# Taking the attention chunks two at a time beside the logits, with four chunk places on two load queues and a shorter float64 conversion

## Chip, cores and metric

One core of one Trainium2 chip runs the whole program. The metric is device microseconds (us) of one execution; lower is better. The quoted time is the median of three timed executions; the trace comes from one further execution, which the hardware profiler recorded.

## What is computed

Three stages, each fed by the one before it. In the first, 8 batches x 8 heads of 576 positions x 64 go through linear attention with decay. In the second, the 4608 tokens of width 512 go through a gated layer with 2048 hidden units. In the third, the tokens are spread over 32 slots (softmax down the tokens), the slots go through 8 small two-layer networks, and a softmax over the slots gathers the results.

```python
scores = scale * np.matmul(q, k.transpose(0, 1, 3, 2))
ret = scores * Dmat            # gamma**(i-j) for i >= j, else 0
x = np.matmul(ret, v)          # -> [4608, 512]
h = x @ w_in;  g = h * (1.0 / (1.0 + np.exp(-1.702 * h)));  y = g @ w_out
logits = y @ phi
d = softmax(logits, over tokens);  slot_input = d.T @ y
slot_out[e] = np.maximum(slot_input[e] @ w1[e], 0.0) @ w2[e]
out = softmax(logits, over slots) @ slot_out
```

`w_in` and `w_out` reach the kernel as float64, everything else as float32.

## The kernel before

**Blocks and chunks.** The tokens go in 12 blocks of 384 (NB). A block needs six attention chunks of 64 positions (C); a chunk covers all 8 heads of one batch, and there are 72. `load_chunk` brings a chunk's q, k and v in two 256 KB DMAs, both issued by SP, into one of three `pack` tiles in turn. `chunk` then works through it: `chunk_out` multiplies on TensorE (tile `Op`), scales on VectorE (`xs`) and splits the result into a rounded and a rest part of `x` (ScalarE L205, GpSimd L206); `state` carries the running k-v product (`St`, eight small matmuls, then two VectorE products into the next pack); after that the pack's place is loaded anew for the chunk three further on, and `scores` computes the masked scores of the next chunk (`Sp`, eight small matmuls, two VectorE products). Op, Sp and St matmuls have 64 output rows each, and run in pairs.

**A block.** For each of 16 slices `fc` of the hidden units, `main_fc` does 12 matmuls of 128x384 into `hp` (L328; the three of a rounded-and-rest product, four times), ScalarE applies the gate (L330), and `turn_fc` transposes on VectorE (L351). After eight slices, 16 DMAs of 96 KB on SP regroup the transposed values into `nat` (L357). `logits_group` adds four slices' logits in four matmuls of 32 output rows each (`Lg`, L364), `softmax_part` (`lt`, `dp`) and `slots_part` (`Sg`, 12 matmuls of 32 output rows, L412) finish the block before. Blocks 1 to 11 are a loop over fc; while block n's matmuls run, the chunks of block n+1 are put in at fc 0, 2, 5, 8, 10 and 12.

**The start.** Block 0's order is the string START: T loads a chunk, A works one through, I converts a slice of w_in (`load_w_in`), O converts two of w_out and folds them with phi into `Wp` (`make_wp`), M is a slice of block 0. A float64 value is turned into a float32 by bit operations on its two halves: scale the upper half on ScalarE, shift the lower by 29 (L277, L295), shift-and-or the two (L278, L296), and put the sign back (L279 for w_in; for w_out ScalarE's Sign L293 and a product L297). The raw values go through a ring of eight places, six in `early_raw` and two in `raw`.

**The order on each engine** is not the order of the code: the instructions are put in order by a scheduler with its own clock when the program is built, so the program text says only which operations exist and what they depend on. Every engine then runs its own list in order, and SP issues its DMAs in order.

**The end.** In the last blocks SP fetches w1 and w2 (33 MB) into places that become free; then come the two layers and the result.

Of the kernel before, what the change touches and what calls it, by code (L numbers as in the profile page):

```python
# [42 lines left out]
NPACK = 3  # L43
# [67 lines left out]
def tile_kernel(ctx, tc, qkv, w_in, w_out, phi, w1, w2, consts, out):  # L111
# [45 lines left out]
    for i in range(NPACK):  # L157
        t = pa.tile([128, 7, NP, C], F32, name=f"pack{i}", bufs=1)
        pool.memset(t[0:C, 0:KN], 0.0)
        pool.memset(t[C:128, KTA:7], 0.0)  # L160
        packs.append(t)
# [75 lines left out]

    def chunk_items(n):
# [3 lines left out]
        chunk_at = CHUNK_AT_LAST if n == LAST else CHUNK_AT  # L242
        return [(chunk_at[i], lambda g=g: chunk(g)) for i, g in enumerate(range(n * NB // C, (n + 1) * NB // C))]
# [10 lines left out]
    def load_raw(src, rows):  # L254
        i = count[0]
        count[0] += 1
        if i % 8 < 6:
            raw = early_raw[:, i % 8]
        else:
            raw = px.tile([128, 1024], F32, tag="raw", name="raw", bufs=2)  # L260
# [24 lines left out]
    def make_wp(i):  # L285
        r0 = 2 * (i % 2)
        for j in range(2):
# [3 lines left out]
            if wide:  # L291
                bits, sign = wo.bitcast(I32), free
# [436 lines left out]
```

## Time and profile before

| | |
|---|---|
| timed executions | 803.54, 803.67, 805.54 us: median 803.67 |
| profiled execution | 797.39 us, of which the recorded span 795.6 us |
| TensorE busy | 727.0 us, 91% of the span |
| VectorE / ScalarE / GpSimd busy | 49% / 31% / 23% |
| granted TensorE clock, mean | 0.982 |
| DMA | 142.19 MB, 179 GB/s over the span |

The profiled execution took 6.3 us less than the median of the timed ones. Busy shares are means over stages with different limits: the start up to the first `hp` matmul at 55.2 us, block 0 up to 127.9 us, the steady blocks 1 to 10 up to 662.5 us, block 11, and the tail from 713 us.

### The profile page before, as it was taken

How to read it: one execution, taken by the hardware profiler on the slowest of the kernel's cores; microseconds unless marked ns; L12 is line 12 of the kernel's file. 1: busy time of each engine (PE TensorE's matmuls, PEld its weight loads, DVE VectorE, ACT ScalarE, POOL GpSimd, SP SyncE). 2: the span in 40 equal slices, each digit the busy share in tenths (PEclk: the TensorE clock that was granted, in tenths of full speed). 3: DMA queues.
4: the chain of work that ended last, by engine and by line, in shares of the span. 5: the costliest groups of instructions: out<-in, count | busy, mean ns of one | idle time of the engine just before them, and what ended most of it. 6: DMA issues, size and time to landing. Idle time of an engine off the chain costs nothing.

```text
span 795.6 us, 18020 instructions
## 1 busy us (share of the span) xinstructions
PE 727.0 (91%) x7288; PEld 589.8 (74%) x7288; DVE 391.0 (49%) x1152; ACT 245.4 (31%) x479; POOL 186.2 (23%) x255
## 2 busy tenths in 40 slices
PE   3359999999999999999999999998998999997994
PEld 3247788788788878887888788878877798772453
DVE  3999964545445535454454454543543542222223
ACT  2446552323123223231132232411311323431323
POOL 5664661121221121212221212121122110001000
PEclk9999899999999999999999999999999999998997
DMA  9998867575355644744555447435544559898978
GB/s 230 283 297 247 266 168 187 128 157 130 80 122 122 135 106 106 159 114 96 119 125 132 111 105 160 116 85 119 134 97 99 124 126 324 278 379 341 408 307 325
DMA packets 78003, 142.19 MB, mean 179 GB/s; under 512 B 10720, under 2 KB 52960, under 8 KB 77920
## 3 DMA queue, kind: packets, MB, share of 16 engines
q1 hardware_dynamic: 75616, 136.85, 62.8%
q10 hardware_dynamic: 2304, 4.20, 1.5%
q8 instruction: 57, 0.93, 0.5%
q14 instruction: 26, 0.21, 0.1%
HBM read 92.77 MB, written 13.63 MB: 134 GB/s over the span
## 4 chain that ended last, share of the span: by engine, by line
PE 63%; SPq 15%; DMA 9%; DVE 9%; issue 3%; ACT 1%; POOL 0%; DVEq 0%; POOLq 0%; ACTq 0%
PE hp L328 38%; SPq L357 13%; DMA pack<-in_qkv_dram 8%; PE Sg L412 4%; PE Lg L364 4%; PE Op L197 2%; PE Sp L184 2%; PE h_ps L589 2%; PE so_ps L653 2%; PE St L223 1%; DMA early_raw<-in_moe_w_in_dram 1%; PE op L671 1%; DVE early_raw L278 1%; SPq L171 1%; PE St L224 1%
## 5 line engine op out<-in xcount | busy, mean ns | idle before, releaser
L328 PE MATMUL hp<-x,w 128*128 128x384 f32 x2304 | 445.3, 346 | 2.2 <-ACT x L205 2.2
L328 PEld LDWEIGHTS hp<-x,w 128*128 128x128 f32 x2304 | 399.8, 191 | 32.8 <-issue 10.6
L330 ACT ACTIVATE gT<-hp 128x384 f32<-128x384 f32 x192 | 93.9, 490 | 299.0 <-PE hp L328 297.9
L187 POOL TENSOR_TENSOR kt<-pack,cs 64x256 f32<-64x256 f32 x128 | 83.1, 649 | 215.2 <-DMA pack<-in_qkv_dram 138.8
L351 DVE STREAM_TRANSPOSE ring<-gT 128x128 f32<-128x128 f32 x240 | 55.9, 284 | 127.1 <-ACT gT L330 127.1
L351 DVE STREAM_TRANSPOSE pre<-gT 128x128 f32<-128x128 f32 x288 | 65.4, 281 | 81.3 <-ACT gT L330 77.9
L206 POOL TENSOR_TENSOR x<-xs,x 128x256 fp32r<-128x256 f32 x72 | 56.4, 783 | 195.9 <-ACT x L205 195.1
L197 PEld LDWEIGHTS Op<-pack 128*64 128x64 f32 x576 | 42.2, 144 | 37.4 <-issue 23.8
L205 ACT CAST x<-xs 128x256 fp32r<-128x256 f32 x72 | 29.1, 405 | 126.3 <-DVE xs L204 126.1
L183 PE MATMUL Sp<-pack 128*64 128x64 f32 x576 | 51.9, 233 | 16.9 <-DMA pack<-in_qkv_dram 11.4
L197 PE MATMUL Op<-pack 128*64 128x64 f32 x576 | 53.3, 236 | 12.0 <-DVE pack L189 12.0
L183 PEld LDWEIGHTS Sp<-pack 128*64 128x64 f32 x576 | 43.2, 146 | 18.9 <-issue 11.5
L223 PE MATMUL St<-pack,kt 128*64 128x64 f32 x512 | 47.2, 234 | 9.4 <-DVE pack L227 7.8
L184 PE MATMUL Sp<-pack 128*64 128x64 f32 x576 | 50.3, 233 | 5.6 <-DMA pack<-in_qkv_dram 5.6
L198 PE MATMUL Op<-pack 128*64 128x64 f32 x576 | 51.4, 236 | 0.0
L223 PEld LDWEIGHTS St<-pack,kt 128*64 128x64 f32 x512 | 38.7, 146 | 14.5 <-POOL kt L187 8.9
L364 PE MATMUL Lg<-gT,Wp 128*32 128x384 f32 x384 | 46.5, 502 | 2.5 <-DVE Wp L312 2.5
L184 PEld LDWEIGHTS Sp<-pack 128*64 128x64 f32 x576 | 42.3, 146 | 8.0 <-DMA pack<-in_qkv_dram 7.7
L224 PE MATMUL St<-pack,kt 128*64 128x64 f32 x512 | 44.8, 234 | 0.0
L198 PEld LDWEIGHTS Op<-pack 128*64 128x64 f32 x576 | 41.6, 145 | 0.7 <-DVE pack L190 0.5
L189 DVE TENSOR_TENSOR pack<-Sp,cs 64x256 f32<-64x256 f32 x72 | 30.6, 424 | 19.7 <-PE Sp L184 13.9
L224 PEld LDWEIGHTS St<-pack,kt 128*64 128x64 f32 x512 | 37.6, 147 | 2.6 <-issue 2.6
(125 smaller groups left out, 644.4 us busy)
## 6 DMA issues: line engine op xcount, KB each, us to landing
pack<-in_qkv_dram SPq DMA_DIRECT2D x144, 256.0 KB, 4.7
wx<-in_moe_w_dram SPq DMA_DIRECT2D x56, 512.0 KB, 8.6
nat<-pre SPq DMA_DIRECT2D x192, 96.0 KB, 2.2
nat<-ring SPq DMA_DIRECT2D x160, 96.0 KB, 2.2
out_dram<-ob SPq DMA_DIRECT2D x18, 512.0 KB, 3.4
early_raw<-in_moe_w_in_dram SPq DMA_DIRECT2D x13, 512.0 KB, 9.9
early_raw<-in_moe_w_out_dram SPq DMA_DIRECT2D x11, 512.0 KB, 7.4
wo_dram<-ring ACTq DMA_DIRECT2D x16, 256.0 KB, 6.2
```

The costliest lines, as they stand in the source:

```text
L183: pe.matmul(Sp[C:128, p, :], t[:, KTA, p], t[:, Q0, p], start=True, stop=True)
L184: pe.matmul(Sp[0:C, p, :], t[:, KTB, p], t[:, Q1, p], start=True, stop=True)
L187: pool.tensor_tensor(kts[g % 2][r0:r0 + C, h], t[r0:r0 + C, KN], ksc[r0:r0 + C, cb, :].unsqueeze(2).to_broadcast([C, NP, D]), op=ALU.mult)
L197: pe.matmul(Op[0:C, p, :], t[:, V0, p], t[:, Q0, p], start=True, stop=True)
L198: pe.matmul(Op[C:128, p, :], t[:, V1, p], t[:, Q1, p], start=True, stop=True)
L223: pe.matmul(s_[0:C, p, :], kk[:, 0, p], t[:, V0, p], start=first, stop=True, skip_group_check=True)
L224: pe.matmul(s_[C:128, p, :], kk[:, 1, p], t[:, V1, p], start=first, stop=True, skip_group_check=True)
L328: pe.matmul(hp, wt[fc][:, a, dc, :], b[n][:, dc, :], start=(i == 0), stop=(i == 3 * NDC - 1))
L330: act.activation(gT[n, g][:, fl, :], hp, AF.Gelu_apprx_sigmoid)
L351: dve.transpose(dst[:, c], src[:, c])
L357: sp.dma_start(nat[n][32 * b:32 * b + 32, :, a, hf * HF:(hf + 1) * HF, :], pre[n, hf][32 * a:32 * a + 32, b])
L364: pe.matmul(Lg[n][32 * fl:32 * fl + 32, :], Wp[:, g * GF + fl, :], gT[n, g][:, fl, :], start=(g == 0), stop=(g == NFC // GF - 1))
```

## The change

1. From the third block on, chunks go in pairs: `two_chunks` at fc 4, 8 and 12 replaces the single chunks at six places, and the logits groups move from fc 6, 10, 14 to fc 4, 8, 12, where the pairs stand (LOGITS_AT 2 to 0). A pair's VectorE, ScalarE and GpSimd operations work on both chunks at once (128x512 where there were two of 128x256), the matmuls stay the same in number and size. The order within an item is St of the pair's second chunk, Op of the pair, Sp of the next pair, St.
2. Four places for packs, in two tiles of two; the loads' lower rows go by SP, the upper rows by ScalarE's queue. A pair's two places are loaded anew, four DMAs, once its Op matmuls are done. The zeroing of the first two places moves from GpSimd to VectorE.
3. The sign of a float64 is made by Prelu: with a slope of 2^32 for negative values the scaled upper half gets the exponent bit that the shift turns into the sign. L279 goes for all 16 slices of w_in; Sign and the product L297 go for all 16 of w_out.
4. The ring of raw values has seven places (`raw` one). The last prefetch has nine places in `pw2` and one in `raw`, where it had eight and two.

```diff
-NPACK = 3
+NPACK = 4
-CHUNK_AT = (0, 2, 5, 8, 10, 12)
-CHUNK_AT_LAST = (0, 3, 6, 9, 10, 13)
-LOGITS_AT, SOFTMAX_AT, SLOTS_AT = 2, 1, 4
+CHUNKS_AT = (4, 8, 12)
+LOGITS_AT, SOFTMAX_AT, SLOTS_AT = 0, 1, 4
...
         sp.dma_start(t[0:C, KN * PC:7 * PC], qkv[g, 0:C])
-        sp.dma_start(t[C:128, 0:KTA * PC], qkv[g, C:128])
+        act.dma_start(t[C:128, 0:KTA * PC], qkv[g, C:128])
...
+    def two_chunks(k):
+
+        g = 2 * k + 1
+        last = g + 1 == NT // C
+        if not last:
+            scaled_keys(g + 1)
+            state(g)
+        out_of_two(k)
+        if not last:
+            scores_of_two(k + 1)
+            state(g + 1)
+            scaled_keys(g + 2)
+        for ahead in (g + 3, g + 4):
+            if ahead < NT // C:
+                load_chunk(ahead)
...
-            act.activation(w, w, AF.Copy, scale=2.0 ** -112)
+            act.activation(w, w, AF.Prelu, scale=2.0 ** -112, alpha=2.0 ** 32)
             dve.tensor_scalar(lower, lower, 29, None, op0=ALU.logical_shift_right)
-            dve.scalar_tensor_tensor(lower, upper, 3, lower, op0=ALU.logical_shift_left, op1=ALU.bitwise_or)
-            dve.scalar_tensor_tensor(upper, upper, -2147483648, lower, op0=ALU.bitwise_and, op1=ALU.bitwise_or)
+            dve.scalar_tensor_tensor(upper, upper, 3, lower, op0=ALU.logical_shift_left, op1=ALU.bitwise_or)
...
-                act.activation(sign, upper.bitcast(F32), AF.Sign)
-                act.activation(wo, upper.bitcast(F32), AF.Copy, scale=2.0 ** -112)
+                act.activation(upper.bitcast(F32), upper.bitcast(F32), AF.Prelu, scale=2.0 ** -112, alpha=2.0 ** 32)
...
-                (pool if how["mul"][i] else dve).tensor_tensor(wo, wo, sign, op=ALU.mult)
```

**On TensorE, in a steady block**, the row of before around a logits group of block 5. `Lg` is the logits group, `hp` a slice of the block, Sp, Op and St are chunk matmuls (Op's L197 and L198, Sp's L183 and L184).

```order
L183 MATMUL Sp<-pack_93 64x64
L184 MATMUL Sp<-pack_93 64x64
L328 MATMUL hp<-x,w 128x384 x24
L364 MATMUL Lg<-gT,Wp 32x384 x4
L328 MATMUL hp<-x,w 128x384 x24
L197 MATMUL Op<-pack_93 64x64
L198 MATMUL Op<-pack_93 64x64
```

The same engine after the change, between the pairs of fc 4 and fc 8 (L387 is `hp`, L423 the logits group, L279 and L280 are St, L201 Op).

```order
L387 MATMUL hp<-x,w 128x384 x14
L423 MATMUL Lg<-gT,Wp 32x384 x3
L279 MATMUL St<-packs_93,kt_106 64x64
L280 MATMUL St<-packs_93,kt_106 64x64
L279 MATMUL St<-packs_93,kt_106 64x64
L280 MATMUL St<-packs_93,kt_106 64x64
L279 MATMUL St<-packs_93,kt_106 64x64
L280 MATMUL St<-packs_93,kt_106 64x64
L279 MATMUL St<-packs_93,kt_106 64x64
L423 MATMUL Lg<-gT,Wp 32x384
L280 MATMUL St<-packs_93,kt_106 64x64
L201 MATMUL Op<-packs_98 64x64
```

The group of four is now cut in three and one with St matmuls between. At the pair of fc 4 another group stands within the slot matmuls `Sg` (L471):

```order
L387 MATMUL hp<-x,w 128x384 x11
L471 MATMUL Sg<-nat,dn 32x512 x6
L423 MATMUL Lg<-gT,Wp 32x384 x4
L471 MATMUL Sg<-nat,dn 32x512 x6
L201 MATMUL Op<-packs_98 64x64
```

Before, the 12 stood together, with hp ahead and Op behind.

**On SP**, the loads of one and a half steady blocks before (L171 and L172 a pack's two halves, L357 the 16 regrouping DMAs):

```order
L357 DMA nat<-pre 32x3x256 x16
L171 DMA pack_93<-in_qkv_dram 64x1024
L172 DMA pack_93<-in_qkv_dram 64x1024
L171 DMA pack_96<-in_qkv_dram 64x1024
L172 DMA pack_96<-in_qkv_dram 64x1024
L172 DMA pack_99<-in_qkv_dram 64x1024
L171 DMA pack_99<-in_qkv_dram 64x1024
L357 DMA nat<-ring 32x3x256 x16
```

and after, where SP issues a pair's two lower halves as one row x2 and L416 is the regrouping (the upper halves stand on ScalarE, ahead of the pair's L245 CAST):

```order
L172 DMA packs_98<-in_qkv_dram 64x1024 x2
L416 DMA nat<-pre 32x3x256 x16
L172 DMA packs_93<-in_qkv_dram 64x1024 x2
L172 DMA packs_98<-in_qkv_dram 64x1024 x2
L416 DMA nat<-ring 32x3x256 x16
L172 DMA packs_93<-in_qkv_dram 64x1024 x2
L416 DMA nat<-pre 32x3x256 x16
L172 DMA packs_98<-in_qkv_dram 64x1024 x2
```

One load of a block still stands behind the 16 regrouping DMAs; the other halves are no longer in this list.

**On VectorE, in the start**, before (L277, L278, L279 convert w_in, L283 is the rest part, L226, L227 and L189, L190 are the chunks' products):

```order
L204 TENSOR_TENSOR xs<-Op,cs 128x256
L277 TENSOR_SCALAR early_raw<-early_raw 128x512
L278 SCALAR_TENSOR_TENSOR early_raw<-early_raw 128x512
L279 SCALAR_TENSOR_TENSOR early_raw<-early_raw 128x512
L226 TENSOR_TENSOR pack_96<-St,cs 64x256
L227 TENSOR_TENSOR pack_96<-St,cs 64x256
L189 TENSOR_TENSOR pack_96<-Sp,cs 64x256
L190 TENSOR_TENSOR pack_96<-Sp,cs 64x256
```

and after (L339 and L340 convert, L344 is the rest part):

```order
L216 TENSOR_TENSOR xs<-Op,cs 128x256
L339 TENSOR_SCALAR early_raw<-early_raw 128x512
L282 TENSOR_TENSOR packs_93<-St,cs 64x256
L283 TENSOR_TENSOR packs_93<-St,cs 64x256
L340 SCALAR_TENSOR_TENSOR early_raw<-early_raw 128x512
L196 TENSOR_TENSOR packs_93<-Sp,cs 64x256
L197 TENSOR_TENSOR packs_93<-Sp,cs 64x256
L344 TENSOR_TENSOR w<-early_raw,w 128x512
```

Each slice has one pass fewer between the chunk's products. Up to the `xs` of chunk 5 this list held 7 L279, 8 L278, 9 L277, 6 L295 and 4 L296; after the change it holds 7 L340, 7 L339, 4 L354 and 3 L355, which are L278, L277, L295 and L296 of before.

## Rows read from the trace of the kernel before

**Rows 1.** The page's first two parts: busy time of TensorE and its granted clock in tenths, in 40 slices of the span.

```profile
PE 727.0 (91%) x7288; PEld 589.8 (74%) x7288; DVE 391.0 (49%) x1152; ACT 245.4 (31%) x479; POOL 186.2 (23%) x255
...
PE   3359999999999999999999999998998999997994
...
PEclk9999899999999999999999999999999999998997
```

**Rows 2.** Windows by stage: stretch, its length, busy us of each engine (instructions), granted clock, DMA share, GB/s.

```profile
0.00:14.00 14.00, 5.08 (x64) 4.23 (x64) 2.27 (x5) 1.61 (x2) 8.21 (x18) 1.00 0.87 188
14.00:60.00 46.00, 21.22 (x254) 18.47 (x255) 43.90 (x72) 20.81 (x37) 28.70 (x25) 1.00 1.05 294
60.00:128.00 68.00, 65.07 (x797) 54.75 (x796) 57.61 (x130) 38.51 (x72) 38.16 (x38) 0.95 0.78 233
128.00:662.50 534.50, 522.66 (x5283) 440.11 (x5282) 251.46 (x860) 141.12 (x279) 108.27 (x172) 0.99 0.53 122
662.50:713.00 50.50, 50.50 (x310) 40.52 (x309) 11.26 (x25) 19.30 (x34) 0.00 (x0) 1.00 0.91 328
713.00:795.60 82.60, 62.45 (x587) 31.68 (x585) 24.46 (x63) 24.07 (x57) 2.83 (x3) 0.91 0.87 345
```

**Rows 3.** All that TensorE waited for in the steady blocks (128 to 662.5 us): total us, times, longest.

```profile
PE Sp L183 <- DMA pack<-in_qkv_dram: 7.4, 9, 1.5
PE Sp L184 <- DMA pack<-in_qkv_dram: 4.4, 6, 0.8
```

**Rows 4.** The chain of waits at one such place, 364 to 387 us (start, us, what).

```profile
364.50 0.20 PE Op L197
365.19 0.47 SPq L171
365.71 4.09 DMA pack<-in_qkv_dram
369.81 0.47 DVE pre L351 x2
370.30 0.64 SPq L357
...
381.47 0.55 SPq L171
382.12 4.00 DMA pack<-in_qkv_dram
386.16 0.27 PE Sp L184
```

**Rows 5.** Windows of the places with the clock at half, columns as in rows 2.

```profile
80.40:87.20 6.80, 6.29 (x25) 4.50 (x25) 6.71 (x14) 4.28 (x8) 4.94 (x6) 0.50 0.99 360
548.00:551.40 3.40, 3.40 (x12) 3.40 (x12) 0.37 (x1) 0.28 (x1) 1.95 (x3) 0.50 0.41 87
602.60:606.00 3.40, 3.40 (x16) 3.28 (x13) 0.84 (x2) 0.00 (x0) 1.77 (x4) 0.50 0.92 193
```

**Rows 6.** TensorE's timeline ahead of these three: start, us, what, and in brackets the idle time before it.

```profile
80.91 1.49 PE L364 MATMUL Lg<-gT,Wp 128*32 128x384 f32 x4 [2.46 <-DVE Wp L312]
...
545.72 0.30 PE L183 MATMUL Sp<-pack 128*64 128x64 f32 x2 [1.51 <-DMA pack<-in_qkv_dram]
546.78 0.27 PE L184 MATMUL Sp<-pack 128*64 128x64 f32 x1 [0.76 <-DMA pack<-in_qkv_dram]
```

**Rows 7.** Groups of instructions of the start (0 to 140 us): total us, mean ns.

```profile
L297 POOL TENSOR_TENSOR ring<-ring 128x512 f32<-128x512 f32 x14 | 20.0, 1445 | 14.8 <-ACT ring L293 7.8 <-DVE raw L295 2.4 <-DVE Wp L312 2.3
L279 DVE SCALAR_TENSOR_TENSOR early_raw<-early_raw 128x512 int32<-128x512 int32 x13 | 10.7, 822 | 0.1
L295 DVE TENSOR_SCALAR early_raw<-early_raw 128x512 int32<-128x512 int32 x11 | 10.4, 942 | 0.1
L278 DVE SCALAR_TENSOR_TENSOR early_raw<-early_raw 128x512 int32<-128x512 int32 x13 | 9.9, 759 | 0.4 <-ACT early_raw L276 0.3
L296 DVE SCALAR_TENSOR_TENSOR ring<-ring,early_raw 128x512 int32<-128x512 int32 x11 | 8.8, 815 | 1.0 <-ACT ring L294 1.0
L277 DVE TENSOR_SCALAR early_raw<-early_raw 128x512 int32<-128x512 int32 x13 | 7.4, 570 | 2.3 <-DMA early_raw<-in_moe_w_in_dram 2.3
L276 ACT ACTIVATE early_raw<-early_raw 128x512 f32<-128x512 f32 x13 | 8.8, 674 | 16.7 <-DMA early_raw<-in_moe_w_in_dram 15.6 <-DMA pack<-in_qkv_dram 1.0
L160 POOL MEMSET pack<- 64x768 f32 x3 | 2.2, 732 | 0.1
```

**Rows 8.** Timelines of VectorE and then of TensorE around the first `hp` matmul.

```profile
54.27 0.42 DVE L204 TENSOR_TENSOR xs<-Op,cs 128x256 f32<-128x256 f32 x1
...
55.19 0.69 PE L328 MATMUL hp<-x,w 128*128 128x384 f32 x1 [2.15 <-ACT x L205]
```

**Rows 9.** TensorE's timeline at a run of 12 `hp` and a whole logits group behind it, a chunk's eight Op matmuls, a run of 24 `hp`, a single logits matmul, and the 12 of `Sg` (32-row and 64-row matmuls are recorded in two passes each: a whole group as 8, a single logits matmul as 2, `Sg` as 24).

```profile
344.33 2.36 PE L328 MATMUL hp<-x,w 128*128 128x384 f32 x12
346.62 0.85 PE L364 MATMUL Lg<-gT,Wp 128*32 128x384 f32 x8
347.40 2.35 PE L328 MATMUL hp<-x,w 128*128 128x384 f32 x12
349.69 0.27 PE L197 MATMUL Op<-pack 128*64 128x64 f32 x1
...
350.20 0.28 PE L223 MATMUL St<-pack,kt 128*64 128x64 f32 x2
...
372.57 4.44 PE L328 MATMUL hp<-x,w 128*128 128x384 f32 x24
...
376.94 0.85 PE L364 MATMUL Lg<-gT,Wp 128*32 128x384 f32 x8
...
662.79 0.83 PE L364 MATMUL Lg<-gT,Wp 128*32 128x384 f32 x2
663.56 0.62 PE L328 MATMUL hp<-x,w 128*128 128x384 f32 x2
...
361.72 2.78 PE L412 MATMUL Sg<-nat,dn 128*32 128x512 f32 x24
364.43 0.27 PE L197 MATMUL Op<-pack 128*64 128x64 f32 x1
```

**Rows 10.** The chunk loads of the page's part on DMA issues: count, KB each, median us from issue to landing.

```profile
pack<-in_qkv_dram SPq DMA_DIRECT2D x144, 256.0 KB, 4.7
```

More of the change, by code (lines that the diff above doesn't have):

```diff
@@ L156, in tile_kernel @@
     packs = []
[L157 to L161, printed above, removed]
+    for i in range(NPACK // 2):
+        two = pa.tile([128, 2, 7, NP, C], F32, name=f"packs{i}", bufs=1)
+        for j in range(2):
+            own = pool if i else dve
+            own.memset(two[0:C, j, 0:KN], 0.0)
+            own.memset(two[C:128, j, KTA:7], 0.0)
+            packs.append(two[:, j])
+        both = [*both, two] if i else [two]
     kts = []
@@ L201, in chunk_out @@
             xh[n], xl[n] = x[:, 0], x[:, 1]
-        cols_ = slice(off, off + C)
-        xs = pa.tile([128, NP, C], F32, tag="xs", name="xs")
-        dve.tensor_tensor(xs, Op, osc, op=ALU.mult)
-        act.copy(xh[n][:, :, cols_], xs)
-        pool.tensor_tensor(xl[n][:, :, cols_], xs, xh[n][:, :, cols_], op=ALU.subtract)
+        return xh[n], xl[n]
+    def chunk_out(g):
+        n, off = divmod(g * C, NB)
+        Op = ps.tile([128, NP, C], F32, tag="r", name="Op", bufs=3)
+        out_products(packs[g % NPACK], Op)
+        hi, lo = (x[:, :, off:off + C] for x in x_of(n))
+        xs = pa.tile([128, NP, C], F32, tag="xs", name="xs", bufs=1)
+        dve.tensor_tensor(xs, Op, osc, op=ALU.mult)
+        act.copy(hi, xs)
+        pool.tensor_tensor(lo, xs, hi, op=ALU.subtract)
@@ new lines, in scores_of_two, with out_of_two @@
+    def scores_of_two(k):
+        two = both[k % 2]
+        Sp = ps.tile([128, 2, NP, C], F32, tag="r", name="Sp", bufs=3)
+        for j in range(2):
+            score_products(two[:, j], Sp[:, j])
+        for q, r0 in ((Q0, C), (Q1, 0)):
+            rows = slice(r0, r0 + C)
+            dve.tensor_tensor(two[rows, :, q], Sp[rows], dtab[rows].unsqueeze(1).to_broadcast([C, 2, NP, C]),
+                              op=ALU.mult)
+    wide_xs = []
+    def out_of_two(k):
+        n, off = divmod(2 * k * C, NB)
+        Op = ps.tile([128, 2, NP, C], F32, tag="r", name="Op", bufs=3)
+        for j in range(2):
+            out_products(both[k % 2][:, j], Op[:, j])
+        hi, lo = (x[:, :, off:off + 2 * C] for x in x_of(n))
+        if not wide_xs:
+            wide_xs.append(px.tile([128, 1024], F32, tag="raw", name="raw", bufs=1))
+        xs = wide_xs[0][:, k % 2 * 512:k % 2 * 512 + 512].rearrange("p (a c t) -> p a c t", a=NP, c=2)
+        dve.tensor_tensor(xs.rearrange("p a c t -> p c a t"), Op, osc.unsqueeze(1).to_broadcast([128, 2, NP, C]),
+                          op=ALU.mult)
+        xs = xs.rearrange("p a c t -> p a (c t)")
+        act.copy(hi, xs)
+        pool.tensor_tensor(lo, xs, hi, op=ALU.subtract)
@@ L241, in chunk_items @@
             return []
-        chunk_at = CHUNK_AT_LAST if n == LAST else CHUNK_AT
-        return [(chunk_at[i], lambda g=g: chunk(g)) for i, g in enumerate(range(n * NB // C, (n + 1) * NB // C))]
+        items = [(0, lambda: second_of_two(4 * NT128 + 1))] if n == 2 else []
+        return items + [(CHUNKS_AT[i], lambda k=n * NT128 + i: two_chunks(k)) for i in range(NT128)]
     wt = {}
@@ L256, in load_raw @@
         count[0] += 1
[L257 to L258 removed]
+        if i % 7 < 6:
+            raw = early_raw[:, i % 7]
         else:
[L260 removed]
+            raw = px.tile([128, 1024], F32, tag="raw", name="raw", bufs=1)
         bits = raw.bitcast(I32)
@@ L471, in step @@
         elif x[0] == "O":
-            how["mul"][8 - len(outs)] = x != "Od"
             outs.pop(0)()
@@ L522, in tile_kernel @@
                     att_ctx.close()
-                    for i in range(2):
-                        prefetch(place_in(px, "raw", 2))
+                    prefetch(place_in(px, "raw", 1))
                     pw2 = ctx.enter_context(tc.tile_pool(name="pw2", bufs=NW2, side="right", reuse_waits="tile"))
```

42 lines of the change are left out of this document (24 added, 18 removed).

## Prediction

> **What bounds the kernel now.** I read busy shares first, then windows by stage, then the waits of the engine that fills its stage. TensorE is busy 91% of the span and above 90% in almost every slice between the start and the tail [rows 1]. By stage [rows 2] there are three regimes. From 14 to 60 us VectorE is busy 43.90 of 46.00 us, TensorE only 21.22, and the DMA share is 1.05, so the start is VectorE's, with the transfers close behind. From 60 to 713 us TensorE fills the time: 65.07 of 68.00, 522.66 of 534.50, 50.50 of 50.50. The tail has 20 us of gaps, but its work is not touched by the change, apart from one place more or less for a prefetch.
>
> In the steady blocks the 11.84 us that TensorE is not busy are one kind of wait, the scores `Sp` on a chunk load: 7.4 + 4.4 us [rows 3]. The chain of waits shows why [rows 4]: SP issues the 16 regrouping DMAs from 370.30 on, they hold its list for 11 us, the load behind them goes out at 381.47, lands 4.00 us after its second half is issued, and Sp starts at 386.16. VectorE's 251 and ScalarE's 141 of 534.5 us there [rows 2] bind nothing.
>
> The granted clock was at half, 1.2 of 2.4 GHz, in three stretches before the tail [rows 5]. Ahead of the first TensorE waited 2.46 us, ahead of the second 1.51 + 0.76 us for a chunk load [rows 6]. A stretch of 6.8 us at half loses up to 3.4 us, the two of 3.4 us up to 1.7 each.
>
> **Part by part, against the profiled 797.4 us (span 795.6, 1.8 outside it).**
>
> *The sign by Prelu, and VectorE in the start.* The first `hp` matmul waits for the last x of its block: `xs` of chunk 5 runs at 54.27 and hp starts at 55.19 [rows 8]. Ahead of that `xs` the changed order holds 7 fewer sign passes, 1 fewer L278, 2 fewer L277, 2 fewer L295 and 1 fewer L296 than the order of before. By the mean durations [rows 7] that is 7 x 0.822 + 0.759 + 2 x 0.570 + 2 x 0.942 + 0.815 = 10.4 us. VectorE is 95% busy in the stretch, so up to 10.4 x 0.95 = 9.9 us of it shows. The zeroing that VectorE takes over (four, nearest row 732 ns on GpSimd, so about 3 us) falls in the first 14 us, where it is busy 2.27; it costs nothing there, and up to 3 us if that cover is gone. What is late next is the transfers: at a share of 1.05 they cannot follow at any speed. I take **-9** for the first hp, with bounds 0 (the transfers decide alone) and -10.4.
>
> Behind the first hp, block 0 must get its remaining weights as fast as TensorE asks. VectorE loses nine more L279 (7.4 us) and GpSimd 14 products L297 (20.0 us) [rows 7], so both stay ahead. Of the 2.46 us wait on `Wp` and the 3.4 us that the clock stretch behind it loses [rows 5, 6], together 5.9, the shorter `make_wp` should return a part. I take **-2.5**; bounds 0 and -5.9.
>
> *The order on TensorE in blocks 1 to 10.* All matmuls remain. What changes is how they are cut. Four logits matmuls side by side take 347.40 - 346.62 = 0.78 us, a single one 663.56 - 662.79 = 0.77 us [rows 9]. So a group cut in three and one costs 0.77 us more. The changed order holds 17 such cuts in these blocks, before at most one: +13.1 us. Nine times a logits group stands in the middle of the 12 `Sg`, six on each side. The 12 run as three rounds of four in 364.43 - 361.72 = 2.71 us; six take two rounds, so two sixes take four: one round more, 2.71 / 3 = 0.9 us, nine times +8.1. Against that the runs of hp are longer. A run of 12 takes 346.62 - 344.33 = 2.29 us, a run of 24 376.94 - 372.57 = 4.37 [rows 9], so each run that is joined to another saves 2 x 2.29 - 4.37 = 0.21 us. The changed order starts 87 runs of hp where there were 111: 24 x 0.21 = -5.0. Sum +16; changes between other kinds (Lg to Op or St without hp between, lt now beside hp) save about 27 x 0.09 less some that are already in the 0.21, so I take **+14**, bounds +12 and +17.
>
> *Loads on two queues, four places.* The 11.8 us of waits and the 3.4 us lost to the half clock [rows 3, 5] go if a pair's data is there when its Sp comes. A place is freed by Op, as before. Before, Op ended near 364.95 (0.51 us for eight matmuls [rows 9]), and the two halves had landed at 369.80 [rows 4]: 4.9 us for 512 KB. A pair is 1 MB. If the second half of the bytes rides beside the first, it is 4.9 us again; if it shares the rate, 512 KB more at the 294 GB/s of the start [rows 2] add 1.7 us: 6.6. The shortest room is between the pairs of fc 4 and fc 8. From the prices above: Sp of the pair 1.0, 14 hp 2.6, a cut logits group 1.5, St 0.5, Op 1.0 and their changes, 7.1 us in seven of ten blocks, and 5.2 where fewer hp stand between, in three. So 0 to 1.4 us of wait remain in three blocks, 0 to 4.2 in all. The one load that still stands behind the 16 regrouping DMAs is for the item that comes 13 us later or more. I take -11.8 - 3.4 + 3 = **-12**, bounds -15 and 0.
>
> A rule of the Trainium skill bears on this: "DMA: Bandwidth & Descriptors", section "Issuing engines are not separate DMA queues", says that transfers run on the same 16 DMA engines whichever engine starts them, and that a second issuer saves only the time to issue. No run here shows a second issuer for these loads; the row of the start with its share of 1.05 from one issuer agrees that the engines, not the issuer, can be full. By the rule the 6.6 us would hold, by separate queues the 4.9, and the sum moves by 4 us.
>
> *Wide operations.* A 128x512 product in place of two 128x256: the nearest rows are 128x512 passes of 0.57 to 0.94 us [rows 7] against two `xs` of 0.42 [rows 8], so nothing to 0.1 us each, on engines that are half idle. Behind Sp, though, Op waits for both products of a pair; hp matmuls stand between, as before. ScalarE issues two loads per pair ahead of its copy of x; at half a microsecond each [rows 4] this delays a copy for the next block, with a block's time of slack. If that cover were gone, some 30 pairs x 1 us would show. I take 0. Block 11 and the tail: the last Op comes one slice of 12 hp earlier, so SP's prefetch may start up to 2 us sooner, and nothing is queued on it that TensorE then waits for: 0, bounds -2 and +1.
>
> **Sum.** -9 - 2.5 + 14 - 12 = -9.5 against 797.4: 787.9. The timed median of before stands 6.3 us above its profiled execution; with the same distance the median after is 794, rounded to **793** for the bounds, which lie further on the fast side (the clock stretch, the joined runs) than on the slow. What this measurement can tell from no change I take as 0.3%, 2.4 us: 801.3 to 806.1.
>
> **Rivals.**
>
> *A, all of it works (0.19).* No wait for chunks is left, so no clock loss behind one, and block 0 gets its 5.9 us back: -9 - 5.9 + 13 - 15 = -17, median 787. For it: the waits of rows 3 are all of one kind. Against it: 1 MB at once.
>
> *B, the transfers bound the start (0.20).* A share of 1.05 with VectorE at 95% leaves it open which of them would be late without the other, and the raw ring has one place less. Then hp moves by 4 us and the clock stretch stays: -4 + 14 - 12 = -2, median 802. Against it: ahead of the last x stand seven slices of w_in, four of w_out and seven chunks, 512 KB each, with the constants some 9.9 MB; 188 GB/s up to 14 us and 294 GB/s from there bring them by 39 us [rows 2].
>
> *C, the other side: the pair's load is late in every block (0.16).* Place: Sp of fc 8. With the start at -11.5, the cuts at +14 and the old waits gone (-11.8, the two clock stretches staying), a new wait of (11.5 - 14 + 11.8) / 10 = 0.93 us per block makes it even, and 2 us per block, a landing at 8 to 9 us behind Op, makes +11: median 814. For it: single halves took a median of 4.7 us with one or two others under way [rows 10], now there are four, and the regrouping DMAs share the engines. Against it: 53% share in these blocks [rows 2].
>
> **How the numbers follow.** My forecast has 0.45, its own range 788 to 800. The range given reaches from A's slower half to short of C: 782 to 808. Faster by over 0.3% hold A, nearly all of the forecast and a third of B: 0.70; within 0.3% most of B and a rest: 0.13; slower C and a little: 0.17.
>
> **What would show it.** The first hp at 46 us instead of 55.2, VectorE still above 90% ahead of it (right for the first term; a DMA share above 1 with VectorE at 80% shows B). TensorE busy time from the first hp of block 1 to that of block 11 up from 522.7 to about 536 with the matmul count unchanged, and single logits matmuls of 0.77 us in it (right for the cuts). The waits of Sp on loads under 4 us, and no half-clock stretch behind them; 10 us or more show C. The forecast is wrong if single logits matmuls between chunk matmuls cost less than between hp, if the regrouping DMAs hold a pair's lower half after all, or if Prelu needs longer than the 674 ns of the scaling copy on ScalarE [rows 7].

## Result, and the profile after

The changed kernel takes 784.75 us (median of four executions, 783.94 to 786.39), the kernel before 803.61 beside it: ratio 0.976, 95% interval 0.974 to 0.979, 18.9 us less. A second group of runs on another chip gave 784.62 against 800.82, ratio 0.980 (0.977 to 0.983). The profiled executions are 797.39 and 784.02, so 13.4 us of it can be followed in the traces.

The windows by stage of the changed kernel, columns as in [rows 2]; the third is blocks 1 to 10, from the first `hp` of block 1 to that of block 11 (127.94 to 662.53 us before, 120.67 to 650.41 now):

```profile
14.00:60.00 46.00, 23.07 (x335) 20.62 (x334) 34.09 (x63) 16.78 (x30) 21.26 (x25) 0.70 1.06 289
60.00:128.00 68.00, 65.16 (x812) 54.89 (x808) 50.47 (x126) 33.67 (x64) 23.32 (x25) 1.00 0.84 240
120.67:650.41 529.74, 520.42 (x5280) 443.72 (x5280) 251.63 (x788) 135.82 (x249) 101.96 (x141) 1.00 0.54 123
```

VectorE is no longer full from 14 to 60 us (34.09 of 46 against 43.90 [rows 2]), the DMA share stays at 1.06. The granted clock of 0.70 comes from two stretches at half, the second of which reaches 3.8 us into block 0 and can cost it up to 1.9 us:

```profile
25.10:42.20 17.10, 10.80 (x160) 9.58 (x160) 13.04 (x26) 4.57 (x8) 8.35 (x10) 0.50 1.06 293
45.60:55.90 10.30, 3.81 (x15) 3.74 (x16) 9.22 (x16) 5.82 (x12) 5.71 (x7) 0.50 1.04 258
```

Behind 56 us no window up to the end of block 11 is at half clock. All that TensorE waited for in blocks 1 to 10 (compare [rows 3]):

```profile
PE Sp L188 <- DMA packs<-in_qkv_dram: 9.2, 10, 1.8
```

Where the 13.4 us come from, by the first `hp` matmuls of the blocks in the two traces:

| stretch | before | after | difference | predicted |
|---|---|---|---|---|
| up to the first hp | 55.19 | 52.09 | -3.1 | -9 |
| block 0 | 72.75 | 68.58 | -4.2 | -2.5 |
| blocks 1 to 10 | 534.59 | 529.74 | -4.9 | +2 |
| block 11 and the tail | 133.1 | 131.8 | -1.3 | 0 |

### The profile page after: what moved, and what is told of

It is laid out like the page before. It is cut to its first block, busy times and chain, and to the rows that moved or that the text cites. A ratio compares the mean times of both kernels' runs of the same rounds, so it can differ in the third digit from the quotient of the medians.

```text
span 782.2 us, 17897 instructions
## 1 busy us (share of the span) xinstructions
PE 716.5 (92%) x7288; PEld 588.8 (75%) x7288; DVE 372.3 (48%) x1050; ACT 230.1 (29%) x433; POOL 155.9 (20%) x209
## 4 chain that ended last, share of the span: by engine, by line
PE 72%; DMA 11%; DVE 2%; SPq 2%; issue 1%; ACT 1%; POOL 0%; DVEq 0%; ACTq 0%; POOLq 0%
PE hp L387 44%; DMA packs<-in_qkv_dram 8%; PE Sg L471 5%; PE Lg L423 5%; DMA wx<-in_moe_w_dram 3%; PE St L279 2%; PE so_ps L710 2%; PE h_ps L646 2%; PE Op L201 2%; PE Sp L189 1%; PE St L280 1%; PE Op L202 1%; PE Sp L188 1%; PE op L728 1%; SPq L416 1%
## 5 line engine op out<-in xcount | busy, mean ns | idle before, releaser
L387 PE MATMUL hp<-x,w 128*128 128x384 f32 x2304 | 432.1, 342 | 11.6 <-ACT x L217 9.9
L387 PEld LDWEIGHTS hp<-x,w 128*128 128x128 f32 x2304 | 397.2, 188 | 28.8 <-ACT x L217 10.1
L183 POOL TENSOR_TENSOR kt<-packs,cs 64x256 f32<-64x256 f32 x128 | 82.5, 644 | 430.9 <-DMA packs<-in_qkv_dram 258.0
L410 DVE STREAM_TRANSPOSE ring<-gT 128x128 f32<-128x128 f32 x240 | 55.9, 284 | 101.7 <-ACT gT L389 101.7
L423 PE MATMUL Lg<-gT,Wp 128*32 128x384 f32 x384 | 67.9, 496 | 1.2 <-DVE Wp L371 1.2
L188 PE MATMUL Sp<-packs 128*64 128x64 f32 x576 | 45.8, 230 | 17.4 <-DMA packs<-in_qkv_dram 17.3
L245 ACT CAST x<-raw 128x512 fp32r<-128x512 f32 x30 | 18.6, 620 | 137.0 <-DVE raw L242 85.0
L201 PEld LDWEIGHTS Op<-packs 128*64 128x64 f32 x576 | 39.2, 142 | 22.9 <-issue 11.6
L188 PEld LDWEIGHTS Sp<-packs 128*64 128x64 f32 x576 | 40.0, 144 | 20.2 <-DMA packs<-in_qkv_dram 9.9
L201 PE MATMUL Op<-packs 128*64 128x64 f32 x576 | 46.2, 231 | 9.4 <-DVE packs L196 9.4
L279 PEld LDWEIGHTS St<-packs,kt 128*64 128x64 f32 x512 | 37.7, 144 | 22.1 <-issue 18.9
L279 PE MATMUL St<-packs,kt 128*64 128x64 f32 x512 | 47.1, 234 | 5.2 <-DVE packs L283 5.0
L228 DVE TENSOR_TENSOR packs<-Sp,cs 64x512 f32<-64x512 f32 x58 | 40.0, 689 | 20.6 <-PE Sp L189 19.9
L280 PE MATMUL St<-packs,kt 128*64 128x64 f32 x512 | 48.0, 235 | 0.0
L189 PE MATMUL Sp<-packs 128*64 128x64 f32 x576 | 46.7, 231 | 0.0
L280 PEld LDWEIGHTS St<-packs,kt 128*64 128x64 f32 x512 | 37.9, 144 | 8.7 <-issue 8.3
L202 PE MATMUL Op<-packs 128*64 128x64 f32 x576 | 44.3, 230 | 0.1
L471 PE MATMUL Sg<-nat,dn 128*32 128x512 f32 x288 | 42.3, 622 | 1.3 <-DMA nat<-ring 1.0
L246 POOL TENSOR_TENSOR x<-raw,x 128x512 fp32r<-128x512 f32 x30 | 38.5, 1285 | 16.0 <-ACT x L245 14.0
L202 PEld LDWEIGHTS Op<-packs 128*64 128x64 f32 x576 | 38.7, 142 | 2.9 <-issue 2.5
```

Of the source, the lines that this page charges most:

```text
L183: pool.tensor_tensor(kts[g % 2][r0:r0 + C, h], packs[g % NPACK][r0:r0 + C, KN], ksc[r0:r0 + C, cb, :].unsqueeze(2).to_broadcast([C, NP, D] ...
L188: pe.matmul(Sp[C:128, p, :], t[:, KTA, p], t[:, Q0, p], start=True, stop=True)
L189: pe.matmul(Sp[0:C, p, :], t[:, KTB, p], t[:, Q1, p], start=True, stop=True)
L279: pe.matmul(s_[0:C, p, :], kk[:, 0, p], t[:, V0, p], start=first, stop=True, skip_group_check=True)
L280: pe.matmul(s_[C:128, p, :], kk[:, 1, p], t[:, V1, p], start=first, stop=True, skip_group_check=True)
L387: pe.matmul(hp, wt[fc][:, a, dc, :], b[n][:, dc, :], start=(i == 0), stop=(i == 3 * NDC - 1))
```

## What the trace of the changed kernel says

**The start.** Timelines of ScalarE, VectorE and TensorE in front of the first hp (start, us, what; in brackets the idle time before; ACTq is a DMA issue from ScalarE's list, L173 a chunk's upper half):

```profile
34.88 0.67 ACT L338 ACTIVATE early_raw<-early_raw 128x512 f32<-128x512 f32 x1
40.59 0.33 ACTq L364 DMA_DIRECT2D wo_dram<-ring  x1
44.83 0.47 ACTq L173 DMA_DIRECT2D packs<-in_qkv_dram  x1
45.34 0.65 ACT L343 CAST w<-early_raw 128x512 fp32r<-128x512 f32 x1 [9.80 <-DMA early_raw<-in_moe_w_in_dram]
...
46.59 1.38 DVE L340 SCALAR_TENSOR_TENSOR early_raw<-early_raw 128x512 int32<-128x512 int32 x1 [6.18 <-ACT early_raw L338]
...
52.09 0.69 PE L387 MATMUL hp<-x,w 128*128 128x384 f32 x1 [9.95 <-ACT x L217]
```

ScalarE does no arithmetic for 9.8 us. Two DMA issues stand in its list in that time: at 40.59 a write of converted w_out to DRAM (`wo_dram`), and at 44.83 the upper half of a chunk load, half a microsecond ahead of the cast. Behind them stands the scaling copy (L338) for which VectorE waits 6.2 us. The cast does not read the transfer in brackets. That is a load of w_in which SP issued at 33.82 (SP's timeline, then the page's part on DMA issues for 33.8 to 34.5 us, with the time to landing last):

```profile
33.82 1.78 SPq L326 DMA_DIRECT2D early_raw<-in_moe_w_in_dram  x2
early_raw<-in_moe_w_in_dram SPq DMA_DIRECT2D x1, 512.0 KB, 10.9
```

It landed at 44.73, and the chunk load went out 0.1 us later. In the trace the two transfers use the same semaphore (the counter by which a transfer reports that it has landed), and the issue waits on it. The issue at 40.59 stands in the same way behind a load of w_out that landed at 40.51. The chunk's place was free before that: TensorE, VectorE and GpSimd had all finished with the chunks by 42.2. So ScalarE's list was held by the landing of a weight transfer, not by the place. This is read from the trace; no run gives the load a semaphore of its own.

**The cuts.** TensorE at the pair of fc 4, where a logits group stands within `Sg`, and then at a group cut in three and one:

```profile
352.36 1.48 PE L471 MATMUL Sg<-nat,dn 128*32 128x512 f32 x10
353.26 0.84 PE L423 MATMUL Lg<-gT,Wp 128*32 128x384 f32 x4
353.68 0.85 PE L471 MATMUL Sg<-nat,dn 128*32 128x512 f32 x4
354.10 0.49 PE L423 MATMUL Lg<-gT,Wp 128*32 128x384 f32 x2
354.36 0.60 PE L471 MATMUL Sg<-nat,dn 128*32 128x512 f32 x2
354.43 0.49 PE L423 MATMUL Lg<-gT,Wp 128*32 128x384 f32 x2
354.75 1.06 PE L471 MATMUL Sg<-nat,dn 128*32 128x512 f32 x8
355.75 0.27 PE L201 MATMUL Op<-packs 128*64 128x64 f32 x1
...
361.52 0.22 PE L279 MATMUL St<-packs,kt 128*64 128x64 f32 x1
361.58 0.28 PE L279 MATMUL St<-packs,kt 128*64 128x64 f32 x2
361.79 0.83 PE L423 MATMUL Lg<-gT,Wp 128*32 128x384 f32 x2
362.55 0.27 PE L280 MATMUL St<-packs,kt 128*64 128x64 f32 x1
```

The 12 Sg and 4 Lg matmuls take 355.75 - 352.36 = 3.39 us together, less than 2.71 + 0.78 apart [rows 9]: the group fills the free columns beside the two sixes, so this cut costs nothing. Its rows overlap in time, Lg from 354.10 beside Sg from 353.68. The Trainium skill, "TensorE: Matmul & The Clock Gate", Part 3 on packing small matmuls, has matmuls on different columns of the array run side by side; the trace agrees, also for matmuls of different length and purpose. The single logits matmul between St takes 362.55 - 361.79 = 0.76 us, as predicted. The step into it from the last St is 361.79 - 361.58 = 0.21 us where St follow each other at 0.06, so a cut costs some 0.9 us in all.

**The waits that are left.** In blocks 3, 6 and 9 the pair of fc 8 waits 1.51, 1.81 and 1.25 us for its load. Those are the three blocks where the room was 5.2 us; 1.4 each was the upper end given. In block 3 the pair's last half landed 6.7 us behind its issue, in block 6 7.3 us, near the 6.6 us that the prediction worked out for halves that share the rate. The pair of fc 8 waits 0.9 us in two more blocks. The other 3.7 us are at the pair of fc 12, in block 8 for instance (SP's and TensorE's timelines):

```profile
518.69 13.21 SPq L416 DMA_DIRECT2D nat<-pre  x16
532.01 4.54 SPq L172 DMA_DIRECT2D packs<-in_qkv_dram  x4
...
537.88 0.27 PE L188 MATMUL Sp<-packs 128*64 128x64 f32 x1 [1.38 <-DMA packs<-in_qkv_dram]
```

The 16 regrouping DMAs hold SP for 13.21 us here (11 before [rows 4]; 10.4 to 13.2 over the blocks of the changed kernel where they stand together), and the 13 us that the prediction counted on is used up.

## Experiments

Each group of runs shared a chip with runs of the kernel before, whose medians were 799.0 (first four), 800.8 (next four) and 801.1 us (last three).

**Prelu alone.** In the kernel before:

```diff
-            act.activation(w, w, AF.Copy, scale=2.0 ** -112)
+            act.activation(w, w, AF.Prelu, scale=2.0 ** -112, alpha=2.0 ** 32)
...
-            dve.scalar_tensor_tensor(upper, upper, -2147483648, lower, op0=ALU.bitwise_and, op1=ALU.bitwise_or)
```

and likewise in `make_wp`.

> The kernel before with part 3 alone (sign by Prelu in both conversions, Od written O); chunks, loads and logits as before. Theory 1 (VectorE holds the start, and in the changed kernel the chunk loads on ScalarE's queue took the gain away): here all chunk loads are on SP, so the first hp comes at 46 to 48 us instead of 55.2 and the time falls by 7 to 9 us, to about 795 to 797 against 803.6. Theory 2 (the transfers hold the start): the first hp comes at 52 us as in the changed kernel, the time is 799 to 801.

Measured 793.4 us, ratio 0.993 (0.989 to 0.996), 5.6 us less. The first hp comes at 52.53, block 1 at 123.37. Window of the start:

```profile
14.00:52.00 38.00, 16.20 (x224) 13.62 (x224) 28.71 (x54) 13.55 (x24) 16.75 (x16) 0.53 1.07 312
```

VectorE is busy 28.71 of 38 us, so the passes are gone and it no longer sets the pace, but the chunk loads are on SP and hp is still at 52.5. The first hp is where theory 2 has it, the gain lies between the two theories (7 to 9 us, and 3 to 5). ScalarE's timeline shows a cause that neither names:

```profile
31.78 5.32 ACTq L302 DMA_DIRECT2D wo_dram<-ring  x2
37.15 0.65 ACT L281 CAST w<-raw 128x512 fp32r<-128x512 f32 x1 [9.44 <-DMA early_raw<-in_moe_w_out_dram]
...
43.58 5.03 ACTq L302 DMA_DIRECT2D wo_dram<-ring  x2
48.65 0.40 ACT L205 CAST x<-xs 128x256 fp32r<-128x256 f32 x1 [6.62 <-DMA raw<-in_moe_w_out_dram]
```

No chunk load stands in ScalarE's list here, but the writes to `wo_dram` do. The second of each two waited for a load of w_out on SP that landed at 36.70 and at 48.21, and ScalarE stood still for 9.4 and 6.6 us; VectorE waited 8.5 us for it. So the run does not show the transfers by themselves to be next.

**The change without Prelu.**

```diff
-            act.activation(w, w, AF.Prelu, scale=2.0 ** -112, alpha=2.0 ** 32)
+            act.activation(w, w, AF.Copy, scale=2.0 ** -112)
...
+            dve.scalar_tensor_tensor(upper, upper, -2147483648, lower, op0=ALU.bitwise_and, op1=ALU.bitwise_or)
```

with Sign and the product L297 back too.

> The changed kernel with the old conversion of the float64 weights (parts 1, 2 and 4 alone). If the changed kernel's gain ahead of block 1 (7.3 us by the two profiles) is Prelu's, the first hp comes at 55 us or later, block 0 takes 72 us again, and the time is 791 to 793 against 784.8. If it comes from the four places and the second queue, the time stays within 2 us of 784.8.

Measured 800.3 us, ratio 1.003 (1.000 to 1.006): all of the gain is gone. The first hp comes at 54.77 and block 0 takes 80.84 us, 8 more than before the change; blocks 1 to 10 take 531.81. In block 0:

```profile
70.00:90.00 20.00, 13.17 (x134) 10.83 (x131) 19.73 (x39) 11.49 (x22) 12.10 (x11) 0.85 0.86 268
```

VectorE is full and TensorE at 13.17 of 20 us. TensorE is at half clock for 15.5 us of this block 0, 6.8 us before; that alone can make 4.4 of the 8 us. The other three parts make the start slower by themselves (seven raw places instead of eight, and loads in ScalarE's list, are what they change there; the run doesn't separate the two). Prelu pays for that and is worth some 16 us here (medians of two chips), not the 5.6 it is worth alone.

**Single chunks' loads on SP.** On the changed kernel:

```diff
-    def load_chunk(g):
+    def load_chunk(g, upper=sp):
...
-        act.dma_start(t[C:128, 0:KTA * PC], qkv[g, C:128])
+        upper.dma_start(t[C:128, 0:KTA * PC], qkv[g, C:128])
...
-                load_chunk(ahead)
+                load_chunk(ahead, act)
```

> The changed kernel with both halves of every single chunk's load on SP; only the pairs' loads from the third block on use ScalarE's queue. Theory 1 (a chunk load at the head of ScalarE's list kept it 9.8 us from the conversion behind it, and VectorE 6.2 us with it): the first hp moves from 52.1 to 46 to 48 us, the time to 779 to 781. Theory 2 (the transfers, share 1.06, hold the start): first hp at 51 to 53 us, time within 1.5 us of 784.8.

Measured 786.1 us, 780.6 to 791.4: no gain that shows. But the first hp moved:

```profile
45.15 0.45 PE L387 MATMUL hp<-x,w 128*128 128x384 f32 x1 [2.40 <-ACT x L217]
...
60.00:100.00 40.00, 36.71 (x473) 31.00 (x472) 34.13 (x81) 23.30 (x45) 16.93 (x18) 1.00 1.04 316
```

It stands at 45.15, 10.0 us ahead of before, and ScalarE's list had eaten 7. In the four traces with these loads on SP it stands at 43.3 to 45.2, in four with them on ScalarE (the changed kernel twice, logits apart, pairs at other places) at 51.4 to 52.4. The 10.0 us are near the 10.4 us of VectorE work in the prediction, but VectorE is busy only 23.90 of the 31 us from 14 to 45 here, so the agreement is no proof of that term. Then block 0 takes 72.78 instead of 68.58 us with the DMA share at 1.04 up to 100 us, so that block 1 begins only 2.7 us earlier (117.93), and block 1 loses another 1.5. From the first hp of block 11 to the end it takes 134.5 us instead of 131.8, with a half-clock stretch of 6.8 us at 705 where the changed kernel has one of 3.4 at 708, and nothing is left. Both theories hold, one behind the other.

**Logits apart from the pairs.** On the changed kernel `LOGITS_AT` is 2 instead of 0.

> The changed kernel with the logits groups back at fc 6, 10 and 14, away from the pairs: 15 fewer groups cut in three and one, no Sg cut, 19 more runs of hp. By the prediction's prices (0.77 us a cut, 0.9 us a cut Sg, 0.21 us a run) TensorE would save 11.6 + 9 - 4 = 16.6 us: 768. By what the changed kernel's trace shows (a Lg group inside Sg costs nothing of its own, a cut 0.86 us, a run some 0.33 us) it saves 12.9 - 6.3 - 1.5 = 5 us: 780, less what chunk waits change.

Measured 787.2 us, 784.4 to 793.4, no less than the changed kernel on other chips; both forecasts, 768 and 780, missed. In blocks 1 to 10, TensorE busy and then its waits:

```profile
120.13:648.70 528.57, 514.78 (x5280) 437.79 (x5279) 250.71 (x788) 136.07 (x249) 101.84 (x141) 1.00 0.55 124
...
PE Sp L188 <- DMA packs<-in_qkv_dram: 13.6, 22, 1.6
```

Busy time falls by 520.42 - 514.78 = 5.6 us, where the prices read from the changed kernel gave 5 and those of the prediction 16.6; the 514.78 hold a half-clock stretch of 3.4 us (at 416.5), up to 1.7 us more. The waits rise from 9.2 to 13.6: without the cuts, less work stands between two pairs. The 1.2 us that these blocks still gain are lost behind them, where block 11 and the tail take 135.4 us instead of 131.8.

**The changed kernel again,** without an edit.

> The changed kernel itself, on the chip of the following three. It should lie at 783 to 788 us with a spread of a few us, and 10 to 19 us below the kernel before. If the kernel before loses part of its time to half-clock stretches that come and go from execution to execution behind its chunk waits, the changed kernel's times spread less than those of before (12 us on the last chip).

784.6 us, 783.1 to 786.9, against 797.3 to 805.2 for the kernel before (eleven executions to its six). It does spread less. Block 1 begins at 119.99, blocks 1 to 10 take 529.15.

**Pairs' loads on SP too.**

```diff
-        act.dma_start(t[C:128, 0:KTA * PC], qkv[g, C:128])
+        sp.dma_start(t[C:128, 0:KTA * PC], qkv[g, C:128])
```

> The changed kernel with both halves of every chunk load on SP, pairs too. Theory 1 (transfers run on the same engines whoever issues them; the gain in blocks 1 to 10 comes from the four places and the longer distance between load and use): Sp's waits there stay at 8 to 14 us in all, blocks 1 to 10 take 528 to 532 us, and with the start as in start_sp the time is within 2 us of the changed kernel. Theory 2 (the second queue is what makes the loads early): the halves behind the 16 regrouping DMAs come 10 us late once a block, Sp waits rise by 10 to 30 us and the time by as much.

Measured 787.8 us, 780.7 to 791.3. Block 1 begins at 115.90, but blocks 1 to 10 take 540.97 us, with 13.8 us of waits and two stretches of 3.4 us at half clock. Landing of the loads, this kernel and then the changed one:

```profile
packs<-in_qkv_dram SPq DMA_DIRECT2D x112, 256.0 KB, 4.8
...
packs<-in_qkv_dram ACTq DMA_DIRECT2D x56, 256.0 KB, 5.3
packs<-in_qkv_dram SPq DMA_DIRECT2D x56, 256.0 KB, 4.7
```

The second issuer makes no load land faster. The Trainium skill, "DMA: Bandwidth & Descriptors", section "Issuing engines are not separate DMA queues", which the prediction cites, has it so. What the second issuer saves is a place in SP's list behind 16 regrouping DMAs. Beside the run with single chunks' loads on SP (530.32 us for the same blocks) this one trace is 10.7 us longer: 4.5 us are waits, and of the 6.4 us by which TensorE is busy longer up to 3.4 are the half clock. The waits rose by less than theory 2's 10 to 30 us and the blocks took longer than theory 1's 532, so neither holds as it was put. The medians differ by 1.7 us on different chips, so the size in time stays open.

**Two edits together:** single chunks' loads on SP, `LOGITS_AT` 2.

> Two edits on the changed kernel together: single chunks' loads on SP alone, and the logits groups at fc 6, 10 and 14. If both small gains of the traces add (block 1 begins 2.7 us earlier with the first; blocks 1 to 10 take 1.2 us less with the second), 780 to 782; if the waits of Sp on loads, 13.6 us with the logits moved, take it back, as the changed kernel.

781.9 us, ratio 0.976 (0.973 to 0.980), 2.7 us under the changed kernel on the same chip, their intervals overlapping; 780 to 782 was expected. Waits of Sp in blocks 1 to 10: 16.1 us.

**More bytes in the start.** On the changed kernel:

```diff
+    extra = pd.tile([NFC // 2, 128, 512], F32, name="extra")
...
+        sp.dma_start(extra[i], w1[i, 0:128, 0:512])
```

> The changed kernel with eight further transfers of 256 KB in the start, one with each pair of w_out slices, from DRAM to DRAM and read by nobody; nothing is left out of the computation. Theory 1 (the transfers hold the start, their share is 1.04 to 1.07): 2.1 MB at 290 GB/s are 7.2 us, so block 1 begins 5 to 8 us later and the time is 790 to 793. Theory 2 (VectorE or the order on ScalarE holds it): block 1 begins at most 2 us later, the time stays within 2 us.

785.3 us against 784.6: within 2 us. In the trace the first hp comes at 57.41 (5.3 us later than in the changed kernel), block 1 at 124.45 (3.8 later). This trace is the slowest of its four executions (788.4 us). The bytes delay the first hp by most of their 7.2 us and block 0 makes part good; in the median next to nothing is left. ScalarE's list is in this run too. The copy below had its input at 41.6 us, and ScalarE stood still for 5.5 us ahead of it, until a write to `wo_dram` went out. That one had waited for the landing of one of the added transfers, which nobody reads:

```profile
45.80 0.40 ACT L217 CAST x<-xs 128x256 fp32r<-128x256 f32 x1 [5.47 <-DMA extra<-in_moe_w_dram]
```

That the transfers hold the first hp fits, at least in part by way of that list; that they alone hold the start doesn't.

**Pairs at fc 3, 7 and 12.** What was left in blocks 1 to 10 was cuts, short runs and waits at pairs that stand close. The smallest edit against all three, first with the two edits above:

```diff
-CHUNKS_AT = (4, 8, 12)
-LOGITS_AT, SOFTMAX_AT, SLOTS_AT = 0, 1, 4
+CHUNKS_AT = (3, 7, 12)
+LOGITS_AT, SOFTMAX_AT, SLOTS_AT = 2, 1, 4
```

> The changed kernel with single chunks' loads on SP, logits at fc 6, 10 and 14, and the pairs at fc 3, 7 and 12 in place of 4, 8 and 12. The list of TensorE then has the pairs 4 and 5 slices apart (before 1 to 4), 104 runs of hp where the changed kernel has 118 and the version with only the first two edits 137, and no cut groups but 3. Theory (what is left in blocks 1 to 10 is cut groups, entries into runs, and waits where two pairs stand close): the waits of Sp on loads fall from 16 us to under 5, 33 fewer runs save 33 x 0.33 = 11 us against the version with two edits, together 765 to 772. If the waits come from the load behind the 16 regrouping DMAs and not from the distance, they stay above 10 us and the time is 775 or more.

Measured **755.7 us**, 752.6 to 758.3, ratio 0.944 (0.940 to 0.948) to the kernel before: faster than both kernels and than the 765 to 772 expected. Blocks 1 to 10 and their waits:

```profile
116.29:621.64 505.35, 503.97 (x5279) 435.86 (x5279) 252.57 (x793) 134.59 (x249) 102.55 (x141) 1.00 0.57 130
...
PE Sp L188 <- DMA packs<-in_qkv_dram: 1.2, 3, 0.5
```

Against the version with two edits busy time falls from 515.61 to 503.97, 11.6 us where 33 runs at 0.33 us gave 11 (up to 1.7 of the 11.6 are a half-clock stretch of 3.4 us in that version), and the waits from 16.1 to 1.2. Block 11 and the tail take 133.8 us, 0.8 more than in that version.

**The same places, nothing else.**

> The changed kernel with CHUNKS_AT = (3, 7, 12) and nothing else: distance alone, with 14 groups still cut and all ten Sg cut. Waits of Sp in blocks 1 to 10 under 4 us instead of 9, 25 fewer runs of hp at 0.33 us: 8 us less. Time 784.6 - 5 - 8 - 1 = 770 to 774. If the prices of a run or of a wait are wrong, it stays above 778.

767.2 us, 766.7 to 768.0, ratio 0.959 (0.956 to 0.962). Blocks 1 to 10:

```profile
120.95:631.53 510.58, 510.58 (x5279) 440.81 (x5279) 250.40 (x793) 134.54 (x249) 102.45 (x141) 1.00 0.57 128
```

There is no wait at all, and busy time is 9.8 us less than in the changed kernel (8 expected; 10 logits groups are cut between chunk matmuls here, 16 there, so this is no clean price of a run). One line of numbers is worth some 17 us (medians of two chips).

**The kernel before again.**

> The kernel before, profiled once more. Its first profile took 797.4 us, 6.3 below its timed median on that chip. If its executions differ by half-clock stretches behind chunk waits, this trace, if it takes 800 us or more, has more or longer stretches at half clock after 100 us than the first (6.8 us), and TensorE's work without them is the same within 1 us.

Timed 798.9 us, 794.8 to 803.0; its profile took 794.8 us, again at the fast end. It has the half-clock stretches of the first at the same places:

```profile
79.70:86.50 6.80, 6.06 (x24) 4.39 (x24) 6.71 (x13) 4.21 (x8) 4.92 (x6) 0.50 0.95 334
547.30:550.70 3.40, 3.40 (x13) 3.40 (x12) 0.41 (x1) 0.20 (x1) 1.95 (x3) 0.50 0.22 53
601.90:605.30 3.40, 3.40 (x11) 3.40 (x12) 0.84 (x2) 0.00 (x0) 1.83 (x3) 0.50 0.87 181
```

So the stretches are the rule and not the accident, and what makes most executions of this kernel 4 to 8 us longer than its two profiled ones is not shown by any trace here.

## Why the prediction was right, and where not

It said 793, 782 to 808, faster: measured 784.75. The direction held; the size was 18.9 us where 10.6 were forecast, nearer to rival A (787).

- **First hp, -9: mis-sized, -3.1.** The step that failed is "ScalarE issues two loads per pair ... I take 0": it looked at the pairs in the steady blocks, where the copy has a block's slack, and not at the single chunks of the start, where a load in ScalarE's list stands ahead of the conversion and, together with a write to `wo_dram`, kept it waiting 9.8 us. With the loads off that list hp comes at 45.15, near the 46 predicted. Rival B named the transfers and put the first hp at -4, and its sign is there: a DMA share of 1.06 with VectorE busy 34.09 of 46 us. They do bear on it, since what ScalarE's list waited for was the landing of one; but with the same share of 1.06 and the loads on SP hp came 7 us earlier, so they did not hold it at 52 us by themselves.
- **Block 0, -2.5: measured -4.2.** The wait on `Wp` fell from 2.46 to 1.2 us and the half-clock stretch behind it is gone; the clock at half up to 55.9 us took up to 1.9 us back. Without that it would be close to the bound of 5.9.
- **The order on TensorE, +14: measured about +1.** The sign that was given, TensorE busy for 536 us, did not come. Busy time in blocks 1 to 10 fell from 522.66 to 520.42; with up to 3.4 us for the half clock taken out of before, the work grew by 1.2. Several terms were mis-sized. The nine cut Sg were put at +8.1 and cost nothing, because the logits group ran beside them. A joined run was put at 0.21 us from the length of runs alone. The change into a run was left out; in the kernel before it takes 0.15 us from the last Sp to hp (344.18 to 344.33 [rows 9]), where Sp follow each other at 0.06:

  ```profile
  344.12 0.22 PE L184 MATMUL Sp<-pack 128*64 128x64 f32 x1
  344.18 0.22 PE L183 MATMUL Sp<-pack 128*64 128x64 f32 x1
  ...
  350.41 0.61 PE L374 MATMUL lt<-Lp,sum4r 128*128 128x384 f32 x2
  350.95 0.27 PE L224 MATMUL St<-pack,kt 128*64 128x64 f32 x1
  ```

  So it is some 0.3, and 24 of them -7 instead of -5. The two `lt` matmuls of a block stood between St before, 0.54 us up to the next St, and stand in a run of hp now, where two take 0.35: another -1.9 in ten blocks. The cut groups at 0.77 were a little low. With the 0.1 us that each logits group within Sg gains these terms give some +3, and about 2 us stay unexplained. The experiment with the logits apart is nearer to prices from the trace: 5.6 us measured (up to 7.3 without its half-clock stretch), 5 by the prices that its expectation read there and 16.6 by the prediction's.
- **Loads, -12: measured -6.** The half clock of 3.4 us is gone, as said. The waits fell from 11.8 to 9.2 and not to 3: the three blocks with 5.2 us of room cost 4.6 of the 4.2 given as the upper end, and the loads behind the regrouping, waved through at "13 us later or more", cost most of the rest, since that list takes up to 13.2 us by itself now. The 9.2 us stay short of the 10 that would have spoken for rival C, and the pair of fc 8 was late by over 1 us in three blocks, not in every one. The start's row that the prediction calls one issuer's holds ScalarE's writes to `wo_dram` too; loads from one issuer alone stand beside those from two in the experiment above.
- **Wide operations, tail: 0** held within a microsecond or so (-1.3 from block 11 on).
- **From profile to median:** the 6.3 us between them before were carried over to after, where they are 0.7. This and the terms above (13.4 by the traces instead of 9.5) make up the 8 us. On the second chip the difference of medians was 16.2.

Errors of opposite sign, the start and the loads too good by 6 each and TensorE's order too bad by 13, nearly met in the middle. That the sum came within 8 us is luck; what the parts show is that the direction of the start, of block 0 and of the loads was right and the price of the order wrong.

## What to carry to other kernels

A DMA issue that may have to wait belongs in the list of an engine that has nothing else to do; in the list of an engine that computes, its wait is everyone's wait behind it (9.8 us here, though with the loads moved what came next took the gain back). Look not only at its place: here the place was free, and the issue stood behind an unrelated transfer with which it shares a semaphore. Where an engine is full with small matmuls of several kinds, count runs and cuts, not matmuls: the same matmuls of blocks 1 to 10 kept TensorE busy 522.7 us before, 520.4 us after the change and 504.0 us with the pairs spaced out, by their order (3.4 us of the first figure being the half clock at most). And look how far apart the consumers of a load stand in the engine's final list rather than in the code; here moving two numbers by one gained about as much as the whole change.

## What was not expected of the hardware

Matmuls of 32 output rows from two different groups, 512 and 384 long, ran beside each other: 16 of them in 3.39 us. Prelu with a scale took 684 ns for 128x512, the copy before 674 [rows 7]:

```profile
L338 ACT ACTIVATE early_raw<-early_raw 128x512 f32<-128x512 f32 x14 | 9.5, 684 | 6.3 <-DMA early_raw<-in_moe_w_in_dram 5.8 <-ACT gT L389 0.4
```

It brought no table load of its own: both traces have 27 on ScalarE.
